# Retention and a squared-ReLU feed-forward in one kernel: groups of two batches, weight transfers issued closer together, and early masks on VectorE

## The chip, the cores and the metric

The kernel runs on one core of a Trainium2 chip. The metric is the device time of one execution in microseconds. Before the change it is 292.26 us, the median of three runs (291.97 to 292.5). The profiled execution, from which all lines below come, spans 290.6 us.

## The reference

Eight batches of eight heads are put through a causal retention: scores of q and k are multiplied by a mask that decays with the distance of two positions, and the result is multiplied with v. The heads of a token are then laid side by side into a row x of 512 numbers, and x goes through two matrix products with relu squared between them.

```python
batch, n_heads, seq, head_dim = (8, 8, 576, 64)
n_tokens, d_model, d_ff = (4608, 512, 2048)

scores = scale * np.matmul(q, k.transpose(0, 1, 3, 2))
gamma = 1.0 - 2.0 ** (-5.0 - np.arange(H))
rel = pos[:, None] - pos[None, :]
Dmat = np.where(rel >= 0, gamma[:, None, None] ** rel[None, :, :], 0.0)
ret = np.matmul(scores * Dmat, v)

x = ret.transpose(0, 2, 1, 3).reshape(B * S, H * D)
h = x @ w_in
r = np.maximum(h, 0.0)
out = (r * r) @ w_out
```

## The kernel before

A sequence of 576 positions is four full chunks of 128 rows and a tail of 64; the tails of two batches share one unit of 128 rows. The kernel so has 36 units, taken two at a time as 18 groups. A group's retention works within the chunk (scores `psc`, mask, times v) and adds what earlier chunks left in a state `R` of 128 x 256 numbers. `psS` holds the sums of k times v from which the next state is made: `Rm` at half a chunk, then `R` at its end, multiplied by the decay of 128 positions. The sum of both parts, `psO`, times a row decay is `xT`, the input of the feed-forward: `ph` (x times w_in), `rl` (relu), `gT` (square), `po` (times w_out). From group 2 on the second product is done with seven block products instead of eight, with sums of blocks of gT (`gS`) and differences of blocks of w_out (`wT`).

```python
    units = []
    for bp in range(B // 2):
        for b in (2 * bp, 2 * bp + 1):
            units += [("full", b, c) for c in range(4)]
        units.append(("tail", 2 * bp, 4))
```

So one batch's chunks follow one another, and a group is mostly two chunks in a row of one batch. The states of the two are updated one after the other, because the second needs the first:

```python
            def fr0(s=s, u=u, c0=c0):
                ... Rm = psS[:, 0] (+ R of unit u - 1)         # 128 x 256, VectorE
            def fr1(s=s, u=u):
                ... stmp = psS[:, 1] + Rm                      # 128 x 256, VectorE
            def fr2(s=s, u=u):
                ... R = stmp * dec128                          # 128 x 256, VectorE
```

The first eight units (two batches, groups 0 to 3) are loaded as pairs, `pair`, and go through another form of the retention, in which casts to fp16 are shared among engines (`kx`, `qx`, `vx`), TensorE transposes k and q (`psT`, copied to `kqT`), and masks `rx` are applied in four halves a group. In groups 0 and 1 (`SHARED`) one half of two is copied from PSUM by ScalarE and multiplied by GpSimd:

```python
                if a and g in SHARED:
                    c = add("ACT", -60 + e, 0.66, fc, deps=[t])
                    reads = ms + [c]
                    ms.append(add("POOL", -60 + e, 0.75, fp, deps=[c]))
                else:
                    ms.append(add("DVE", base + 5 + e, 0.66, fm, deps=[t] + ms))
```

The weights come as eight transfers of 1 MB of fp32, cast to fp16 on the way, w0 to w3 for w_in and w4 to w7 for w_out. GpSimd issues them, between its own computing:

```python
            tile_of["w", i] = nc.gpsimd.dma_start(out=dst, in_=src)
        issue = add("POOL", -70 + i, 1.0, fn, deps=issues[-1:], lag=1.6 if issues else 0.0)
        if not issues:
            gate.setdefault(("vx", 0), []).append(issue)
```

The load of k for unit 4 is made to wait until weight 6 has landed:

```python
            if (name, u) == ("k", 4):
                tc.add_manual_dep(t.ins, tile_of["w", 6].ins.name, ..., reason="the weights come first")
```

The order of instructions on each engine is fixed when the kernel is built, by a list scheduler in the program: `add(engine, key, duration, function, deps, acq)` gives it a task with a rank and an assumed duration. On the chip an engine takes its instructions in that order and waits for what each of them needs. TensorE's idle time at the start is filled with products of a zero tile (`warm`, 28 of them).

In the feed-forward a block is eight ph products of 256 columns, in one of four PSUM buffers; ScalarE takes the relu, and the square is done by ScalarE or by VectorE:

```python
            on_act = g >= STRASSEN and fb in (SQ_ACT if g < last_g - 1 else SQ_LATE)     # STRASSEN = 2, SQ_ACT = 0 to 6
```

The last group is the last full chunk and the last tail, with the tail first. Each unit's output is stored in halves of 256 columns; a tail's half needs two issues of 64 rows, since its rows lie in two batches.

Of the kernel before, what the change touches and what calls it, by code (L numbers as in the profile page):

```python
# [103 lines left out]
def kernel(  # L104
# [21 lines left out]
    for bp in range(B // 2):  # L126
        for b in (2 * bp, 2 * bp + 1):
            units += [("full", b, c) for c in range(4)]
        units.append(("tail", 2 * bp, 4))
# [8 lines left out]
    groups[-1].reverse()  # L138
# [10 lines left out]
    st_pool = ctx.enter_context(tc.tile_pool(name="st", bufs=6))  # L149
# [12 lines left out]
    junk = const.tile([P, 512], FP16, name="junk")  # L162
# [54 lines left out]
    for hp in range(NP):  # L217
# [7 lines left out]
    WARM = 28  # L225
# [5 lines left out]
    LAG = {"w0": 1.2, "k4": 0.7, "q4": 0.5}  # L231
    LAG_T, LAG_O = 1.5, 5.0
    PAIRED = 8
    SHARED = (0, 1)
    FIRST = ["k0", "q0", "v0", "k2", "q2", "v2", "w0", "w1", "w2", "w3", "w4", "w5", "w6", "w7", "k4", "q4", "v4", "k6", "q6", "v6"]
    sched = Schedule(dict(ff=4, prS=1, prO=1, g=3, ld=5, wst=4, kq=7, v16=7, rT=4, x=3, rl=3, o=4, p1=2, u2=2, u4=2,
                          R=6, Rm=6, kqT=6))
# [38 lines left out]

    def add_load(u):
        kind, b, c = units[u]
        for n, (name, src) in enumerate((("k", k), ("q", q), ("v", v))):
            def fn(name=name, src=src):  # L280
                x = ld.tile([P, H, D], FP32, name=f"{name}32", tag=f"{name}32")
                tile_of[name + "32", u] = x
                if kind == "full":
                    nc.sync.dma_start(out=x, in_=src[b, :, c * P:(c + 1) * P, :].rearrange("h p d -> p h d"))
                else:
                    for i in range(2):
                        nc.sync.dma_start(out=x[i * 64:(i + 1) * 64],
                                          in_=src[b + i, :, 512:576, :].rearrange("h p d -> p h d"))
            loaded[name, u] = dma_task(0, 1.2 if loaded else 2.1, fn, acq=("ld",) if n == 0 else ())

    def add_load_pair(name, u):
        b, c = units[u][1:]
        n = "kqv".index(name)

        def fn():
            if name != "q":
                tile_of["stage", u] = stage.tile([P, 2, H, 2 * D], FP32, name="pair", tag="wst")
            x = tile_of[name + "32", u] = tile_of["stage", u][:, n % 2]
            t = nc.sync.dma_start(out=x, in_=(k, q, v)[n][b, :, c * P:(c + 2) * P, :].rearrange("h (p e) d -> p h (e d)", e=2))
            if (name, u) == ("k", 4):  # L300
                tc.add_manual_dep(t.ins, tile_of["w", 6].ins.name,
                                  mybir.DependencyInfo(mybir.DependencyClass.Sync, mybir.DependencyReason.DATA),
                                  reason="the weights come first")
        loaded[name, u] = loaded[name, u + 1] = dma_task(0, 1.81 if loaded else 2.9, fn, acq=("wst",) if name != "q" else (),
                                                         after=2.1 + LAG.get(name + str(u), 0.0))

    issues = []

    def add_weight(i):
# [6 lines left out]
        issue = add("POOL", -70 + i, 1.0, fn, deps=issues[-1:], lag=1.6 if issues else 0.0)  # L316
        if not issues:
            gate.setdefault(("vx", 0), []).append(issue)
# [18 lines left out]

    def quad(out_, lhsT, rhs, row, col, start=True):
        nc.tensor.matmul(out_, lhsT=lhsT, rhs=rhs, start=start, stop=True, skip_group_check=True,  # L339
                         tile_position=(64 * row, 64 * col))  # L340
# [38 lines left out]
    def add_unit_pair(u, base):  # L379
# [29 lines left out]
        for w in gate.get(("vx", u), []):  # L409
            sched.need(w, xs["v"][0])  # L410
# [24 lines left out]
        T["kvx", u] = xs["k"] + xs["v"]  # L435

    def add_ret_pair(g):
# [50 lines left out]
        sched.free("kq", [t])  # L488
        chain = []
        for s in range(2):  # L490
            src = None if s == 0 and not carry else u + s - 1

            def fr1(s=s, src=src):
                r = tile_of["tmp", u + s] = work.tile([P, NP * D], FP32, name="stmp", tag="stmp", bufs=1)
                nc.vector.tensor_tensor(out=r, in0=rT["sum"][s][:, 0:256], in1=tile_of["R", src], op=ALU.add)

            def fr2(s=s, src=src):
                r = tile_of["R", u + s] = st_pool.tile([P, NP * D], FP16, name="R", tag="R")
                x = rT["sum"][s][:, 0:256] if src is None else tile_of["tmp", u + s]
                nc.vector.tensor_tensor(  # L500
                    out=r.rearrange("p (n d) -> p n d", d=D), in0=x.rearrange("p (n d) -> p n d", d=D),
                    in1=dec128.rearrange("p (n o) -> p n o", o=1).to_broadcast([P, NP, D]), op=ALU.mult)
            if src is not None:
                chain.append(add("DVE", base + 5.5 + s, 0.42, fr1, deps=[t] + chain[-1:] + [T["R", src]]))
                T["Rread", src].append(chain[-1])
                sched.free("ff", chain[-1:])
            chain.append(add("DVE", base + (6.5 if u == 0 else 5.6) + s, 0.5, fr2, deps=[t] + chain[-1:], acq=("R",)))
            if src is None:
                sched.free("ff", chain[-1:])
            T["R", u + s], T["Rread", u + s] = chain[-1], []  # L510

        def inter(other):
            for n in range(2):
                for a, b in ((0, 0), (1, 1), (0, 1), (1, 0)):
                    s = a ^ other
                    if s or carry:
                        x = 2 * n + b
                        put2(s, 4 * n + 2 * a + b, tile_of["R", u + s - 1][half(a), half(x)], kqT(s)[half(a), NP + x, :], a)
# [22 lines left out]
        t = add("PE", base + 24, 0.75, fo2, deps=[t, T["R", u]] + ([T["R", u - 1]] if carry else []))  # L541
        for s in range(2):
            sched.free("kqT", [t])
            sched.free("kq", [t])
            if s or carry:
                T["Rread", u + s - 1].append(t)
# [23 lines left out]

    def states(u):

        kind, b, c = units[u]
        if kind == "tail":
            return {0: ("R", u - 5), 1: ("R", u - 1)}
        return {1: ("Rm", u), 0: ("R", u - 1)} if c else {1: ("Rm", u)}
# [37 lines left out]
    def inter(g, u, other):  # L614
        st = states(u)
        for n in range(2):
            for a, b in ((0, 0), (1, 1), (0, 1), (1, 0)):
                c = a ^ other
                if c in st:
                    x = 2 * n + b  # L620
                    put(g, u, c, 4 * n + 2 * a + b, tile_of[st[c]][half(a), half(x)],
# [29 lines left out]
    def out1_deps(g):  # L651
        return [T[x] for u in units_of(g) for x in states(u).values()]

    def after_scores(g, t, key):
        for s, u in enumerate(units_of(g)):
            def fm(s=s, u=u):
                r = tile_of["rT", u] = work.tile([P, 2, NP, 64], FP16, name="rT", tag="rT")
                nc.vector.tensor_tensor(  # L658
# [6 lines left out]
    def after_sums(g, t, key, res):  # L665

        chain = []
        for s, u in enumerate(units_of(g)):
            if u not in full_of(g):
                continue  # L670
            c0 = units[u][2] == 0

            def fr0(s=s, u=u, c0=c0):
                r = tile_of["Rm", u] = st_pool.tile([P, NP * D], FP16, name="Rm", tag="Rm")
                x = tile_of["psS", g][:, 0, cols(s)]
                if c0:
                    nc.vector.tensor_copy(out=r, in_=x)
                else:
                    nc.vector.tensor_tensor(out=r, in0=x, in1=tile_of["R", u - 1], op=ALU.add)

            def fr1(s=s, u=u):
                r = tile_of["tmp", u] = work.tile([P, NP * D], FP32, name="stmp", tag="stmp", bufs=1)
                nc.vector.tensor_tensor(out=r, in0=tile_of["psS", g][:, 1, cols(s)], in1=tile_of["Rm", u], op=ALU.add)

            def fr2(s=s, u=u):
                r = tile_of["R", u] = st_pool.tile([P, NP * D], FP16, name="R", tag="R")
                nc.vector.tensor_tensor(
                    out=r.rearrange("p (n d) -> p n d", d=D), in0=tile_of["tmp", u].rearrange("p (n d) -> p n d", d=D),
                    in1=dec128.rearrange("p (n o) -> p n o", o=1).to_broadcast([P, NP, D]), op=ALU.mult)
            r0 = add("DVE", key + 0.1 + s, 0.42, fr0, deps=[t] + chain[-1:] + ([] if c0 else [T["R", u - 1]]),  # L690
                     acq=("Rm",))
            if not c0:
                T["Rread", u - 1].append(r0)
            r1 = add("DVE", key + 0.2 + s, 0.42, fr1, deps=[r0])
            r2 = add("DVE", key + 0.3 + s, 0.5, fr2, deps=[r1], acq=("R",))
            chain += [r0, r1, r2]
            T["Rm", u], T["R", u], T["Rread", u], T["Rmread", u] = r0, r2, [], r1
        if chain:
            sched.free(res, [chain[-2]])

    def after_outs(g, t1, t2, key):
        us = units_of(g)
        n = len(us)
        for u in us:
# [3 lines left out]
            for name, ru in states(u).values():  # L708
                if name == "R":
                    T["Rread", ru].append(t2)  # L710
                else:
                    sched.free("Rm", [t2, T["Rmread", u]])
# [22 lines left out]
    def add_ret(g):  # L735
# [17 lines left out]
        if joined(g):  # L753
# [6 lines left out]
            def f2():  # L760

                emit_sums(g + 1, "prS")
                emit_out2(g)
# [4 lines left out]
                     deps=[t1] + T["masked", g] + T["masked", g + 1] + sums_deps(g + 1), acq=("prS",))  # L768
# [17 lines left out]
    wT = [const.tile([P, HF, HM], FP16, name=f"wT{i}") for i in range(4)]  # L786
# [36 lines left out]
    def add_ff(g):  # L823
# [10 lines left out]
        for fb in range(NF // nf):  # L834
# [16 lines left out]
            on_act = g >= STRASSEN and fb in (SQ_ACT if g < last_g - 1 else SQ_LATE)  # L851
# [185 lines left out]
    for u in range(NU):  # L1037
        if ("Rread", u) in T:
            sched.free("R", T["Rread", u])
# [33 lines left out]
```

## Time and profile before

| | us |
|---|---|
| time, median of three runs | 292.26 |
| span of the profiled execution | 290.6 |
| TensorE busy | 281.6 |
| VectorE busy | 197.9 |
| ScalarE busy | 183.0 |
| GpSimd busy | 91.4 |
| first ph product starts | 17.88 |
| ph products that need the last quarter of w_in start | 26.77 |
| first ph product of group 2 starts | 54.04 |
| last product ends, by the model | 287.0 |

The profile calls the engines PE (TensorE; PEld is its weight load), DVE (VectorE), ACT (ScalarE), POOL (GpSimd) and SP (SyncE), and POOLq or SPq their queues, which issue transfers. In a group of instructions, out<-in are tile names, and x is a count. The chain of waits follows the work that ended last back to its releasers; in order of time it reads as a diary of what was waited for. Windows give each engine's busy time in a stretch. TensorE's busy time in them includes the warm-up products, and counts a product as busy until its modelled end.

| stretch, us | PE | DVE | ACT | POOL |
|---|---|---|---|---|
| 0 to 10 | 8.64 | 4.32 | 5.45 | 4.86 |
| 10 to 20 | 8.09 | 9.72 | 6.02 | 8.72 |
| 20 to 30 | 9.04 | 6.11 | 5.01 | 3.71 |
| 30 to 40 | 10.00 | 4.94 | 5.27 | 0.00 |
| 40 to 50 | 9.92 | 8.51 | 6.42 | 5.16 |
| 50 to 60 | 9.40 | 8.49 | 4.59 | 5.05 |

### The profile page before, as it was taken

How to read it: one execution, taken by the hardware profiler on the slowest of the kernel's cores; microseconds unless marked ns; L12 is line 12 of the kernel's file. 1: busy time of each engine (PE TensorE's matmuls, PEld its weight loads, DVE VectorE, ACT ScalarE, POOL GpSimd, SP SyncE). 2: the span in 40 equal slices, each digit the busy share in tenths (PEclk: the TensorE clock that was granted, in tenths of full speed). 3: DMA queues.
4: the chain of work that ended last, by engine and by line, in shares of the span. 5: the costliest groups of instructions: out<-in, count | busy, mean ns of one | idle time of the engine just before them, and what ended most of it. 6: DMA issues, size and time to landing. Idle time of an engine off the chain costs nothing.

```text
span 290.6 us, 10028 instructions
## 1 busy us (share of the span) xinstructions
PE 281.6 (97%) x4316; PEld 233.6 (80%) x4316; DVE 197.9 (68%) x427; ACT 183.0 (63%) x351; POOL 91.4 (31%) x125
## 2 busy tenths in 40 slices
PE   8978999999999999999999999999999999999995
PEld 3557755688888888888888888888888888888884
DVE  3895369949384849675968767867767876565632
ACT  5654466486767575867767566666767676747830
POOL 5782035525433334241604251615051500000000
PEclk9999999999999999999999999999999999999999
DMA  7999999999999999997959999969699820201004
GB/s 200 275 192 181 182 300 280 215 204 193 235 173 220 208 167 235 219 214 182 190 135 210 200 192 213 204 170 187 161 182 212 167 74 2 74 2 73 2 0 147
DMA packets 139421, 49.94 MB, mean 172 GB/s; under 512 B 118128, under 2 KB 135024, under 8 KB 139376
## 3 DMA queue, kind: packets, MB, share of 16 engines
q1 hardware_dynamic: 134848, 44.84, 75.1%
q0 software_dynamic: 4224, 4.19, 9.1%
q8 instruction: 34, 0.56, 0.8%
q10 hardware_dynamic: 304, 0.26, 0.3%
q14 instruction: 11, 0.09, 0.1%
HBM read 36.70 MB, written 9.44 MB: 159 GB/s over the span
## 4 chain that ended last, share of the span: by engine, by line
PE 88%; DVE 6%; DMA 3%; ACT 1%; issue 1%; POOL 0%; DVEq 0%
PE ph L841 41%; PE po L933 34%; PE psO L339 4%; PE po L881 3%; DMA w_in<-in_moe_w_in_dram 3%; DVE rx L459 2%; PE warm L248 2%; PE psS L339 2%; PE psc L339 2%; DVE vx L396 2%; DVE R L500 1%; PE psT L417 1%; DVE xT L552 0%; ACT rl L849 0%; POOL rx L466 0%
## 5 line engine op out<-in xcount | busy, mean ns | idle before, releaser
L841 PE MATMUL ph<-xT,w_in 128*128 128x256 f16 x1152 | 140.1, 273 | 1.1 <-DMA w_in<-in_moe_w_in_dram 1.1
L841 PEld LDWEIGHTS <-w_in 128*128 128x128 f16 x1152 | 110.6, 98 | 16.6 <-DMA w_in<-in_moe_w_in_dram 1.9
L849 ACT ACTIVATE rl<-ph 128x512 f16<-128x512 f32 x144 | 84.9, 590 | 57.2 <-PE ph L841 55.8
L859 ACT ACTIVATE gT<-rl 128x512 f16<-128x512 f16 x104 | 65.6, 631 | 3.0
L933 PEld LDWEIGHTS <-gS 128*128 128x128 f16 x512 | 49.5, 98 | 6.1 <-DVE gS L910 0.2
L933 PE MATMUL po<-wT,gS 128*128 128x256 f16 x384 | 52.1, 273 | 0.0
L910 DVE TENSOR_TENSOR gS<-gT,gS 128x512 f16<-128x512 f16 x64 | 32.6, 515 | 13.4 <-ACT gT L859 12.7
L933 PEld LDWEIGHTS <-gT 128*128 128x128 f16 x384 | 37.3, 98 | 4.4
L910 DVE TENSOR_TENSOR gS<-gT 128x512 f16<-128x512 f16 x64 | 33.5, 524 | 10.7 <-ACT gT L859 10.5
L933 PE MATMUL po<-w_out,gT 128*128 128x256 f16 x256 | 34.7, 273 | 0.0
L363 POOL TENSOR_TENSOR v<-v,vdec_full 128x512 f16<-128x512 f32 x24 | 26.4, 1100 | 21.7 <-DMA v<-in_v_dram 12.2
L351 POOL CAST kq<-k 128x512 f16<-128x512 f32 x28 | 19.5, 696 | 42.3 <-DMA k<-in_k_dram 40.6
L351 POOL CAST kq<-q 128x512 f16<-128x512 f32 x28 | 19.1, 682 | 42.3 <-DMA q<-in_q_dram 42.3
L861 DVE TENSOR_TENSOR gT<-rl 128x512 f16<-128x512 f16 x40 | 19.5, 489 | 17.6 <-ACT rl L849 17.2
L956 DVE TENSOR_TENSOR o<-po,u 128x256 f32<-128x256 f32 x31 | 13.0, 420 | 14.8 <-PE po L933 9.6
L719 DVE TENSOR_TENSOR xT<-psO,gam_full 128x512 f16<-128x512 f32 x28 | 18.1, 684 | 6.8 <-PE psO L339 6.8
L946 ACT COPY u<-po 128x256 f32<-128x256 f32 x32 | 11.8, 368 | 17.2 <-PE po L933 17.0
L658 DVE TENSOR_TENSOR rT<-psc,mask 128x512 f16<-128x512 f32 x28 | 18.3, 682 | 3.9 <-PE psc L339 3.9
L933 PE MATMUL po<-w_out,gS 128*128 128x256 f16 x128 | 16.9, 273 | 0.0
L933 PE MATMUL po<-wT,gT 128*128 128x256 f16 x128 | 16.6, 273 | 0.0
L881 PE MATMUL po<-w_out,gT 128*128 128x512 f16 x64 | 15.8, 380 | 0.0
L956 DVE TENSOR_TENSOR o<-po,p 128x256 f32<-128x256 f32 x17 | 7.2, 423 | 12.5 <-ACT u L946 6.5
(81 smaller groups left out, 239.6 us busy)
## 6 DMA issues: line engine op xcount, KB each, us to landing
out_dram<-o SPq DMA_DIRECT2D x31, 256.0 KB, 3.5
k<-in_k_dram SPq DMA_DIRECT2D x24, 256.0 KB, 4.4
q<-in_q_dram SPq DMA_DIRECT2D x24, 256.0 KB, 5.0
v<-in_v_dram SPq DMA_DIRECT2D x24, 256.0 KB, 4.9
pair<-in_k_dram SPq DMA_DIRECT2D x4, 512.0 KB, 5.9
pair<-in_q_dram SPq DMA_DIRECT2D x4, 512.0 KB, 6.0
pair<-in_v_dram SPq DMA_DIRECT2D x4, 512.0 KB, 7.0
w_in<-in_moe_w_in_dram POOLq DMA_DIRECT2D x4, 512.0 KB, 7.7
```

The costliest lines, as they stand in the source:

```text
L339: nc.tensor.matmul(out_, lhsT=lhsT, rhs=rhs, start=start, stop=True, skip_group_check=True, tile_position=(64 * row, 64 * col))
L351: op(out=out_.rearrange("p (n b a d) -> p n b a d", n=2, b=2, a=2), in_=in_.rearrange("p (n a b) d -> p n b a d", n=2, a=2))
L363: nc.gpsimd.tensor_tensor(out=t, in0=tile_of["v32", u], in1=vdec[kind].rearrange("p (h o) -> p h o", o=1).to_broadcast([P, H, D]), op=ALU. ...
L658: nc.vector.tensor_tensor(out=r, in0=tile_of["psc", g][:, :, cols(s)].rearrange("p a (n i) -> p a n i", i=64), in1=mask.rearrange("p (o r ...
L841: nc.tensor.matmul(tile_of["ph", g, fb][:, j, :], lhsT=w_in16[:, m, fi * P:(fi + 1) * P], rhs=tile_of["x", g][:, m, :], start=(m == 0), st ...
L849: nc.scalar.activation(out=t, in_=tile_of["ph", g, fb], func=ACTF.Relu)
L859: nc.scalar.activation(out=t, in_=rl, func=ACTF.Square)
L861: nc.vector.tensor_tensor(out=t, in0=rl, in1=rl, op=ALU.mult)
L881: nc.tensor.matmul(tile_of["po", u], lhsT=tile_of["g", g][:, fi, s * P:(s + 1) * P], rhs=w_out16[:, fi, :], start=(fi == 0), stop=(fi == N ...
L910: nc.vector.tensor_tensor(out=Sx(k, h), in0=in0(h), in1=in1(h), op=op)
L933: nc.tensor.matmul(tile_of["pb", g, bank], lhsT=left(i), rhs=right[:, i, :], start=(start and i == 0), stop=(i == HF - 1), skip_group_chec ...
L956: nc.vector.tensor_tensor(out=o_tile(u)[:, half * HM:(half + 1) * HM], in0=bank(x), in1=tile_of[name, g], op=ALU.add)
```

## The change

From unit 8 on, two batches advance together: a group is the same chunk of two batches, so both states are updated by one instruction of 512 columns. Tails come two units at a time, after each second pair of batches, as groups of their own (8 and 17). The weights' issues get higher rank and shorter lags, the first is tied to the landing of v for unit 0 and no longer follows GpSimd's first product, and k for unit 4 waits for weight 5. All masks of groups 0 and 1 are VectorE's, and in exchange squares of groups 0 and 1 go to ScalarE. The warm-up products become 34 and read a weight tile not yet in use. The last group's order is no longer reversed.

```diff
-        for b in (2 * bp, 2 * bp + 1):
-            units += [("full", b, c) for c in range(4)]
-        units.append(("tail", 2 * bp, 4))
+        bs = (2 * bp, 2 * bp + 1)
+        units += [("full", b, c) for c in range(4) for b in bs] if bp else [("full", b, c) for b in bs for c in range(4)]
+        if bp % 2:
+            units += [("tail", b, 4) for b in (2 * bp - 2, 2 * bp)]
...
-    groups[-1].reverse()
...
-    junk = const.tile([P, 512], FP16, name="junk")
+    wT = [const.tile([P, NF // 2, DM // 2], FP16, name=f"wT{i}") for i in range(4)]
+    junk = wT[3][:, 0:2].rearrange("p f m -> p (f m)")
...
-    WARM = 28
+    WARM = 34
-    LAG = {"w0": 1.2, "k4": 0.7, "q4": 0.5}
+    LAG = {"k4": 0.7, "q4": 0.5}
-    SHARED = (0, 1)
+    SHARED = ()
-                          R=6, Rm=6, kqT=6))
+                          R=5, Rm=2, kqT=6))
...
             if (name, u) == ("k", 4):
-                tc.add_manual_dep(t.ins, tile_of["w", 6].ins.name, ...)
+                behind(t, tile_of["w", 5])
...
-        issue = add("POOL", -70 + i, 1.0, fn, deps=issues[-1:], lag=1.6 if issues else 0.0)
-        if not issues:
-            gate.setdefault(("vx", 0), []).append(issue)
+            if i == 0:
+                behind(tile_of["w", i], tile_of["load", "v", 0])
+        issue = add("POOL", -90 + i, 0.9, fn, deps=issues[-1:] or [loaded["v", 0]], lag=1.0 if issues else 0.0)
...
-            on_act = g >= STRASSEN and fb in (SQ_ACT if g < last_g - 1 else SQ_LATE)
+            on_act = fb in (SQ_ACT if g < last_g - 1 else SQ_LATE)
...
-        for s, u in enumerate(units_of(g)):          # Rm, stmp and R for one unit after the other, 256 columns
...
+        def fr0():                                   # Rm, stmp and R for both units, 512 columns
+            r = tile_of["Rm", g] = st_pool.tile([P, 2, NP * D], FP16, name="Rm", tag="Rm", bufs=2)
+            ...
+        def fr1():
+            r = tile_of["tmp", g] = work.tile([P, 2, NP * D], FP32, name="stmp", tag="stmp", bufs=1)
+            nc.vector.tensor_tensor(out=flat(r), in0=tile_of["psS", g][:, 1], in1=flat(tile_of["Rm", g]), op=ALU.add)
+        def fr2():
+            r = tile_of["R", g] = st_pool.tile([P, 2, NP * D], FP16, name="R", tag="R", bufs=5)
+            decay(flat(r), flat(tile_of["tmp", g]))
```

Where a group has only tails, it makes no psS, and the first product of the joined step before it waits for that group's masks (`first_waits` in the kernel).

In the order of instructions that each engine gets, VectorE has 46 instructions fewer (429 to 383), ScalarE 14 squares more and four copies fewer, GpSimd four products fewer, and TensorE the same products plus the six warm-ups. On SyncE's queue the load of v for unit 6 now stands ahead of the first two stores; before it stood behind the first.

## The prediction

> **What bounds the kernel now.** I read the engine table of the page first, then the chain of waits in order of time, then the waits and the transfers by stretch.
>
> ```profile
> PE 281.6 (97%) x4316; PEld 233.6 (80%) x4316; DVE 197.9 (68%) x427; ACT 183.0 (63%) x351; POOL 91.4 (31%) x125
> ```
>
> TensorE leads, but "97% busy" counts the warm-up products and modelled ends, so I counted work. A 256-column product follows the next after 0.109 us (16 in 1.75 us of the chain), a 512-column one after 0.216 us, a 64x64 one after about 0.0095 us. Products counted in stretches of 10 us at these prices give 8.1 us of work for 20-30, 9.0 for 40-50, 8.1 for 50-60, and 9.7 to 10.2 for nearly every stretch from 60 to 280. So the **steady part is full**: 1008 + 896 products of 0.109 us make 208 of the 228 us from 57.2 to 285.5, and 1680 small ones make 16 more. Only the ramp (0 to 58 us) and the end (after 286 us) have time to give. The chain through the ramp:
>
> ```profile
> 14.26 1.96 DVE vx L396
> 16.27 0.41 PE psS L339 x28
> ...
> 16.95 0.59 ACT rx L463
> 17.62 1.07 POOL rx L466
> 18.73 7.99 DMA w_in<-in_moe_w_in_dram
> 26.77 2.79 PE ph L841 x24
> ```
>
> Columns: start, length, what. The last quarter of w_in lands at 26.7, 8 us after GpSimd issued it, and GpSimd issued it so late because it first multiplied masks (L466). From 26.77 on the chain is TensorE without a gap until 41.5, then TensorE and VectorE in turn, up to here:
>
> ```profile
> 49.28 1.27 DVE vx L396
> ...
> 50.73 1.35 DVE xT L552 x2
> 52.08 1.16 DVE rx L459 x2
> 53.24 0.34 DVE stmp L495
> ...
> 53.61 1.26 DVE R L500
> 54.88 1.21 DVE rx L459 x2
> ...
> 56.13 0.75 PE psO L339 x40
> ```
>
> Here VectorE sets the pace of units 4 to 7. The third view is the SyncE queue's own waits:
>
> ```profile
> SPq L299 <- DMA w_out<-in_moe_w_out_dram: 25.9, 1, 25.9
> ```
>
> The load of k4 stands 25.9 us behind weight 6 and goes out at 34.4. The last is DMA by stretch (the last two columns are share and GB/s):
>
> ```profile
> 23.00:25.00 2.00, 1.74 (x17) 1.34 (x15) 1.12 (x3) 1.00 (x2) 0.70 (x1) 1.00 1.11 140
> 27.00:34.00 7.00, 7.00 (x59) 5.52 (x57) 2.52 (x6) 3.04 (x6) 0.00 (x0) 1.00 1.24 205
> ```
>
> With the weights queued the engines move 205 GB/s; in 23-25 they fall to 140, in 15-17 to 165, and in 35-36 to 89, where neither weights nor loads are queued.
>
> [...]the trace has 0.414 to 0.424 for the 256-wide state updates and 0.68 for the 512-wide masks[...]. [...]L500[...] takes 1.39 us at 12.54, beside GpSimd's masks (11.34 to 13.63), and its like L687 has a median of 0.425. [...]
>
> **The change part by part.**
>
> 1. *Masks of groups 0 and 1.* Four ScalarE copies (4 x 0.59 = 2.4 us) and four GpSimd products (4 x 1.17 = 4.7 us) go; VectorE gets four masks of 0.66 us = 2.6 us. VectorE is 9.7 of 10 us busy in 10-20, so this lies on its path; but without GpSimd's products its updates at 12.54 and 17.81 fall from 1.39 and 1.25 to about 0.43, giving back 1.8 us. The first vx also runs less beside GpSimd (1.23 to about 0.8). The sum is about +0.4 us, and the first ph stays at 17.4 to 17.9.
>
> 2. *Weights.* w0 is issued when v0 has landed, ahead of GpSimd's vx (9.77 to about 8.8). With four GpSimd products gone and the lags shortened, w1 to w3 move from 13.57, 15.59, 18.73 to about 11, 12.5 and 15.4 (the last behind vx of unit 2, which waits for v2 at about 14), the w_out quarters from 20.7-23.7 to about 16-20. Bytes don't shrink: 3.15 MB of loads at 290 GB/s (10.9 us) and 4.19 MB of weights at 203 GB/s (20.7 us), begun at 2.3, end at 33.9 if nothing ever runs dry. What can be won is the lulls: about 0.35 us in 15-17 and 0.75 in 23-25. A quarter takes 2.6 us, so w3, in order, can land at 13.2 + 4 x 2.6 = 23.6 at the earliest. I take 25.2, as [...]the products before it (56 of 0.109 us, 1.3 us of psO, from 17.4) fill TensorE to 24.8 anyway. Gain: 26.8 - 25.2 = **1.6 us**, all on the path.
>
> 3. *k4 behind w5, not w6.* It goes out about 3 to 4 us sooner, the hole at 35-36 closes, and in the order of SyncE's queue v6 now stands ahead of two stores instead of behind one. The chain above waits for v6 (48.9). TensorE lacks about 2.5 us of work in 37-58. I give **0.9 us** to this, with the weight differences wT moved ahead of vx of unit 4, out of the stretch 43-49.
>
> 4. *Squares of groups 0 and 1 on ScalarE.* 14 go from VectorE (0.43 us) to ScalarE (0.63 us): +8.8 us there. With 16 relus of 0.60 that is 18.4 us of ScalarE between about 18 and 37, where it is now busy 10.3 of the 20 us from 20 to 40. Each block of eight ph products (0.87 us) then costs 1.23 us of ScalarE; with four PSUM buffers the last block starts no sooner than the twelfth relu, 18 + 11 x 1.23 + 0.6 = 32.1. TensorE gets there at about 35. It is close, not binding. Cost: **+0.2 us**.
>
> 5. *Two batches in a group.* In each of 12 groups, six updates (2 x 0.41, 2 x 0.42, 2 x 0.52 = 2.7 us) become three of 512 columns (3 x 0.68 = 2.0 us), and the second unit no longer waits for the first. VectorE is freed of 12 x 0.7 = 8 us, but it waits for others there and TensorE is full: **0** on the path. TensorE's small products are the same in number.
>
> 6. *The end.* The last group is now two tails. Each half row-block is stored by two issues of 64 rows. The last was one issue at 287.52 of 0.34 us; two make **+0.4 us**.
>
> 7. *34 warm-up products, not 28*: they fill idle time; 0.
>
> Sum: -1.6 - 0.9 + 0.2 + 0.4 = -1.9; with a little of part 1 left over I write -2.2: 292.26 - 2.2 = about 290.0.
>
> **The rivals.**
>
> *DMA is the true bound of the ramp.* If the slowest DMA engine had no lull, earlier issues change nothing: w1 to w6 land 2.85 us apart (20.1 to 34.4) against 2.6 at the full rate, which speaks for it. The 140 GB/s speaks against it. Then only parts 3 and 6 are left: 291.5 to 292.3.
>
> *ScalarE becomes the bound of the ramp.* If relus and squares in one queue hold PSUM buffers, ph ends no sooner than now (37.2) and the copies of k for unit 4 wait behind them. For it: a quarter of w_in feeds four blocks, two of each group, and so 4.9 us of ScalarE for 2.6 us of transfer; the 16 blocks need 18.4 us, and TensorE wants to be through them in 17.6 (17.4 to 35). Against it: ScalarE may trail by four PSUM buffers. If it binds: 291.5 to 293.
>
> *The steady part gains too.* If freed VectorE time shortened hidden waits, 4 us could come back at most (228 less 208 less 16). For it: quads wait with the release "issue" 43 times, 10.2 us on the weight-load side. Against it: VectorE holds TensorE up for hardly anything after 60 us. It would make 287 to 288.5.
>
> **Range and chances.** The ramp's gain is between 0 and 4 us, the end costs 0.2 to 0.8, the steady part gives -1 to +0.5 either way. Eight in ten: 287.6 to 292.0. Faster by over 2% needs 286.4, that is, all of the ramp and the steady part together: 0.06. Slower by over 2% needs 298.1: only a new wait in every group would do that, 0.02. Within 2%: 0.92.
>
> **What would show it.** Part 2: w3's ph block starts at about 25 instead of 26.77, and no 140 GB/s lull. Part 1: no L466-like row on GpSimd, the update after the second stmp near 0.43 us. Part 3: v6's cast on VectorE starts two to three us before 49.28. Part 4: ScalarE nearly full from 18 to 37; if ph products wait for relus there, it was too much. Part 5: VectorE's busy time near 187 us, ScalarE's near 190, the interval from one psO to the next still about 14.1 us. Part 6: the span ends about 3.5 us after VectorE's last operation instead of 3.1. It is wrong if the time between groups changes, or if the first ph of group 2 (54.04) moves by other than 1.5 to 3.5 us.

## The result, and the profile after

The changed kernel takes **290.75 us**, the median of four runs (290.56 to 290.92), against 292.38 us for the kernel before, run beside it. The ratio is 0.9946, with a 95% interval from 0.9928 to 0.9963. A second comparison, made later, gave 290.70 us and 0.9932 [0.9909, 0.9954]. So the change is worth a little over half a per cent, and the prediction of 290.0 us was 0.75 us too low. The four runs lie within 0.4 us, and the six of the second comparison within 0.3; the 19 of the kernel before in that comparison lie between 291.61 and 294.40.

The engine table of the changed kernel's page (busy time, share of the span of 289.1 us, instructions):

```profile
PE 282.1 (98%) x4322; PEld 234.3 (81%) x4322; DVE 182.4 (63%) x381; ACT 188.2 (65%) x361; POOL 84.1 (29%) x121
```

VectorE lost 15.5 us, GpSimd 7.3, ScalarE gained 5.2, and the span fell by 1.5 us only. TensorE is what it was. The chain of waits shows where the 1.5 us come from (start, length, what):

```profile
10.95 8.72 DMA w_in<-in_moe_w_in_dram
...
19.72 1.49 PE ph L859 x12
...
22.29 5.78 PE ph L859 x52
28.07 0.86 PE po L899 x4
...
52.28 1.75 PE ph L859 x16
54.03 0.68 PE psO L345 x40
```

Set beside the chain of before, two things are gone. The last quarter of w_in is no link any more: only w1 (issued at 10.95) is waited for, and from 19.7 us TensorE works on, with one gap of 0.1 us, until the first po at 28.07. And the VectorE links between 49 and 56 us (vx, xT, rx, stmp, R) have vanished; the stretch up to group 3 is TensorE's alone. The same moments in both kernels, from their traces:

| moment | before | after | difference |
|---|---|---|---|
| first ph | 17.88 | 17.74 | -0.1 |
| first po, behind 80 ph products | 29.56 | 28.07 | -1.5 |
| ph of groups 0 and 1 at their end | 37.39 | 35.90 | -1.5 |
| first ph of group 2 | 54.04 | 52.28 | -1.8 |
| psO of group 3 | 56.13 | 54.03 | -2.1 |
| psO of the last group | 256.62 | 254.44 | -2.2 |
| VectorE's last operation ends | 287.49 | 285.31 | -2.2 |
| span | 290.6 | 289.1 | -1.5 |

The moments are the starts of pieces of the chain; in the repeat of the changed kernel (run 10) the first po came at 28.24 and psO of group 3 at 54.12, so a difference of 0.1 or 0.2 us between two profiles says nothing. Everything is won before 56 us, nothing is won in the 200 us from psO of group 3 to psO of the last group (200.49 before, 200.41 after; the steady part in what follows), and 0.7 us are given back behind VectorE's last operation.

DMA by stretch (window, length, then busy time of PE, PEld, DVE, ACT, POOL, then PEclk, DMA share, GB/s):

```profile
23.00:25.00 2.00, 2.00 (x21) 1.80 (x19) 0.71 (x2) 1.94 (x4) 0.00 (x0) 1.00 1.24 205
27.00:34.00 7.00, 7.00 (x57) 5.31 (x55) 2.41 (x4) 6.84 (x13) 0.00 (x0) 1.00 1.23 215
```

The lull of 140 GB/s at 23-25 us is filled (205), and ScalarE, at 6.84 of 7 us, is nearly full from 27 to 34. Yet no wait of TensorE on a relu appears among its waits. SyncE's queue now waits 21.3 us for a weight ahead of k4 instead of 25.9.

The state updates, from the groups with shapes kept apart (count, then busy time, mean ns, idle time before):

```profile
L445 DVE TENSOR_TENSOR R<-stmp,dec 128x512 f16<-128x512 f32 x12 | 10.0, 831 | 0.4
L705 DVE TENSOR_TENSOR stmp<-psS,Rm 128x512 f32<-128x512 f32 x12 | 8.2, 687 | 0.3
L701 DVE TENSOR_TENSOR Rm<-psS,R 128x512 f16<-128x512 f32 x9 | 6.1, 680 | 0.0
L404 DVE TENSOR_TENSOR vx<-pair,vdec_pair 128x512 f16<-128x512 f32 x4 | 3.2, 791 | 3.0 <-DMA pair<-in_v_dram 3.0
L445 DVE TENSOR_TENSOR R<-stmp,dec 128x256 f16<-128x256 f32 x6 | 2.7, 450 | 0.2
```

Three updates of a group make 0.83 + 0.69 + 0.68 = 2.2 us. The last two rows are the ramp's: vx had a mean of 1369 ns before and R one of 867.

The end (start, length, engine, operation):

```profile
284.89 0.42 DVE L974 TENSOR_TENSOR o<-po,p 128x256 f32<-128x256 f32 x1
282.63 3.83 SPq L833 DMA_DIRECT2D out_dram<-o  x4
```

SyncE issues its last store until 286.46, that is 1.15 us after VectorE's last operation. Before it was done 0.37 us after it. The trace has the two last issues singly: 0.46 and 0.58 us for 64 rows each, where the kernel before has one of 0.34 us, for 128 rows.

### The profile page after: what moved, and what is told of

Same layout as the page of the kernel before. It is cut to its first block, busy times and chain, and to the rows that moved or that the text cites. A ratio compares the mean times of both kernels' runs of the same rounds, so it can differ in the third digit from the quotient of the medians.

```text
span 289.1 us, 9988 instructions
## 1 busy us (share of the span) xinstructions
PE 282.1 (98%) x4322; PEld 234.3 (81%) x4322; DVE 182.4 (63%) x381; ACT 188.2 (65%) x361; POOL 84.1 (29%) x121
## 4 chain that ended last, share of the span: by engine, by line
PE 91%; DMA 3%; issue 2%; POOL 2%; DVE 0%; POOLq 0%; DVEq 0%
PE ph L859 44%; PE po L951 34%; PE po L899 5%; PE psO L345 4%; DMA w_in<-in_moe_w_in_dram 3%; PE psc L345 2%; PE psS L345 2%; PE psT L423 1%; POOL mask L215 0%; POOL vx L404 0%; POOL w_in L319 0%; DVE o L974 0%; POOL mask L207 0%; DVE p L1003 0%; POOL mask L211 0%
## 5 line engine op out<-in xcount | busy, mean ns | idle before, releaser
L877 ACT ACTIVATE gT<-rl 128x512 f16<-128x512 f16 x118 | 74.4, 631 | 3.4
L928 DVE TENSOR_TENSOR gS<-gT 128x512 f16<-128x512 f16 x64 | 30.9, 485 | 12.6 <-ACT gT L877 12.5
L359 POOL CAST kq<-k 128x512 f16<-128x512 f32 x28 | 18.6, 663 | 61.4 <-DMA k<-in_k_dram 60.2
L371 POOL TENSOR_TENSOR v<-v,vdec_full 128x512 f16<-128x512 f32 x24 | 25.4, 1057 | 21.9 <-DMA v<-in_v_dram 20.9
L359 POOL CAST kq<-q 128x512 f16<-128x512 f32 x28 | 18.5, 660 | 30.8 <-DMA q<-in_q_dram 30.6
L879 DVE TENSOR_TENSOR gT<-rl 128x512 f16<-128x512 f16 x26 | 12.8, 492 | 12.6 <-ACT rl L867 11.9
```

Source lines behind the costliest of these rows:

```text
L359: op(out=out_.rearrange("p (n b a d) -> p n b a d", n=2, b=2, a=2), in_=in_.rearrange("p (n a b) d -> p n b a d", n=2, a=2))
L371: nc.gpsimd.tensor_tensor(out=t, in0=tile_of["v32", u], in1=vdec[kind].rearrange("p (h o) -> p h o", o=1).to_broadcast([P, H, D]), op=ALU. ...
L877: nc.scalar.activation(out=t, in_=rl, func=ACTF.Square)
L928: nc.vector.tensor_tensor(out=Sx(k, h), in0=in0(h), in1=in1(h), op=op)
```

## The experiments

All times are compared with the kernel before, run beside them on the same chip; its medians there were 292.43 us for runs 1 to 4, 292.36 for runs 5 to 8, 292.86 for runs 9 and 10, and 292.33 for run 9b. The theory at the start was that of the prediction: the ramp carries the gain, by way of the weights' issues. The rivals were that the grouping of two batches carries it, or that one simpler part of the ramp does. The 34 warm-up products were not tried alone; run 6, which has most of the gain, has 28.

**1. The grouping alone.** The changed kernel with all its ramp taken back:

```diff
-    SHARED = ()
+    SHARED = (0, 1)
-    WARM = 34
+    WARM = 28
-    LAG = {"k4": 0.7, "q4": 0.5}
+    LAG = {"w0": 1.2, "k4": 0.7, "q4": 0.5}
-                behind(t, tile_of["w", 5])
+                behind(t, tile_of["w", 6])
-        issue = add("POOL", -90 + i, 0.9, fn, ..., lag=1.0 if issues else 0.0)
+        issue = add("POOL", -70 + i, 1.0, fn, ..., lag=1.6 if issues else 0.0)     # and its gate on vx of unit 0
-            on_act = fb in (SQ_ACT ...
+            on_act = g >= STRASSEN and fb in (SQ_ACT ...
```

> The changed kernel with every part of the ramp put back (issues and lags of the weights, k4 behind weight 6, masks of groups 0 and 1 shared, their squares on VectorE, 28 warm-up products): what stays is the grouping of two batches, the tails in groups of their own and the last group of two tails. Theory (the gain is all in the ramp, the grouping gives nothing on TensorE's path, the end costs 0.7 us): 0.5 to 0.9 us slower than the kernel before, 292.9 to 293.3; psO of group 3 at about 56.1 and psO of the last full group's successor as far from it as before. Rival (the grouping shortens the steady part by about 1 us, and the ramp brings only the rest): 291.3 or less, with the last product ending about 1 us earlier than before.

Measured: 292.77 us, 1.0009 [0.9995, 1.0023]; the span is 290.9 us, psO of group 3 at 55.56, the steady part 200.77 us. The lull is back:

```profile
15.00:17.00 2.00, 1.38 (x56) 0.94 (x53) 2.00 (x3) 1.07 (x2) 1.56 (x2) 1.00 0.99 148
```

By itself the grouping, which takes 8 us of work from VectorE by the prediction's count, gives nothing: the steady part is no shorter, and the end, 3.74 us behind VectorE's last operation, is 0.6 us longer. That the loss is 0.3 us and not the 0.5 to 0.9 of the theory comes from psO of group 3, which is 0.6 us earlier than in the kernel before although the ramp's edits are out. What moved it was not isolated.

**2. The ramp alone.** The kernel before with all the ramp's edits (those above, the other way round).

> The kernel before with the ramp's parts alone (weights issued early and close, k4 behind weight 5, all masks on VectorE, squares of groups 0 and 1 on ScalarE, 34 warm-up products); units and groups are as before, and so is the last group (tail and full chunk). Theory: the ramp's 2.1 us without the 0.7 us of the end, so about 290.1, 0.6 us faster than the changed kernel. Rival (the grouping carries part of the gain): 291 or more, slower than the changed kernel.

Measured: 291.12 us, 0.9956 [0.9946, 0.9965]. The ramp is as fast as the changed kernel's (psO of group 3 at 54.09), and the last store is issued as soon behind VectorE's last operation as before (0.36 us), though the span ends 0.3 us later behind it (3.40 us). Yet the time is no better than the changed kernel's, since from psO of group 3 to the last it takes 201.46 us, 1.0 us more than before. One wait of TensorE that neither the kernel before nor the changed one has was found (total, times, longest):

```profile
PE po L934 <- DVE gS L911: 0.7, 2, 0.5
```

Its larger part is near 140.7 us, where a sum gS of 1.15 us stands behind six state updates and beside a GpSimd product of v. So by these profiles the grouping is not worthless beside the fast ramp: it makes good up to 1.0 us, and the longer end takes part of that again. How firm that is, run 6 says.

**3. Weight issues and k4 as before, the rest changed.** The issue line, the gate, `LAG` and `behind(t, tile_of["w", 6])` of run 1, with the masks left on VectorE.

> The changed kernel with the weights' issues, their lags and k4 behind weight 6 as before; masks and squares stay as changed. Without GpSimd's mask products the issues still move up a little. Theory (early issue removes the lulls of the transfers, and this is most of the ramp's gain): w0 issued at about 9.8, products of the last quarter of w_in at 25.5 to 26.5, time 291.6 to 292.4. Rival (it is the masks taken off GpSimd that move the weights, the ranks and lags do little): 290.9 to 291.3.

Measured: 291.12 us, 0.9959 [0.9943, 0.9975]; psO of group 3 at 54.12 (54.03 in the changed kernel), no lull between 14 and 33 us (206 GB/s in the mean, 199 to 215 by the microsecond). This fells the theory in its first form. The edits on the issues themselves, and k4 behind w5, are worth 0.1 us of the ramp at most; the changed kernel's own repeat has the same 54.12. The medians differ by 0.4 us, with intervals that overlap.

**4. Masks of groups 0 and 1 shared again, the rest changed.**

```diff
-    SHARED = ()
+    SHARED = (0, 1)
```

> The changed kernel with the masks of groups 0 and 1 shared with ScalarE and GpSimd again; weights and squares stay as changed. Theory (GpSimd's four products of 1.17 us stand between the issues[...], but the new ranks already put most issues ahead of them): the first xT ends about 1 us later, the first weights land about as now, time 291.0 to 291.8. Rival (the masks are the key to the ramp): 292.2 or more, with a lull in the transfers again between 15 and 25 us. ScalarE has four copies more in a stretch where it is nearly full; if that binds, products of groups 0 and 1 wait for relus.

Measured: 294.26 us, 1.0066 [1.0045, 1.0088]; 3.5 us above the changed kernel. The weights kept flowing (206 GB/s at 15-17 us, 201 at 23-25), with the last quarter of w_in landed at 24.76, but the masks came late. TensorE's waits, and the chain:

```profile
PE psO L345 <- POOL rx L481: 1.5, 3, 0.9
```

```profile
12.64 1.82 DVE R L445
14.46 0.80 DVE qx L408
...
15.76 1.53 DVE vx L404
17.29 1.27 DVE xT L573 x2
...
18.70 1.91 PE ph L859 x16
20.61 0.38 PE psc L345 x16
...
21.00 0.70 DVE rx L474
...
21.73 0.59 ACT rx L478
...
23.53 1.16 POOL rx L481
...
24.73 0.58 PE psO L345 x28
```

It was not the issues that the masks of group 1 waited for: GpSimd had issued w5 by 19.0 us and then stood idle for 3.4, until ScalarE's copy. The chain goes back over that copy, VectorE's mask and psc, which in this order comes behind 16 ph products, to VectorE, where R took 1.82 us beside GpSimd's masks (0.42 in run 6) and the first ph so came at 18.70, 1.0 us later than in the changed kernel. Before, the issues waited for the masks; here TensorE does. Runs 3 and 4 with the two kernels make a table of four. The gain is in the step from the left column to the right, and the lower row is harmless only there. (The upper left is the kernel before, which differs from run 3 also in grouping, squares and warm-ups; run 6 makes the upper step with the masks alone, from 292.4 to 291.14.)

| | masks shared with GpSimd | masks on VectorE |
|---|---|---|
| issues as before | 292.4 (292.8 with the grouping, run 1) | 291.12 (run 3) |
| issues closer together | 294.26 (run 4) | 290.75 (the changed kernel) |

**5. The end on two queues.** In the changed kernel the two issues of the last two half row-blocks go out one on SyncE's queue and one on ScalarE's.

```diff
-                eng.dma_start(out=out[r0:r0 + 64, lo:hi], ...)
+                (eng[i] if isinstance(eng, tuple) else eng).dma_start(out=out[r0:r0 + 64, lo:hi], ...)
-                    eng = ("ACT", ...) if d is d11 or d is d22 else ("SP", ...)
+                    eng = ("ACT", ...) if d is d11 else ("SP", ...)
-                    nc.scalar if eng[0] == "ACT" else nc.sync
+                    nc.scalar if eng[0] == "ACT" else nc.sync if lo and u == uA else (nc.sync, nc.scalar)
```

> The changed kernel with the two issues of each of the last two half row-blocks put on two queues, SyncE's and ScalarE's, instead of both on one. Theory (the changed end is 0.7 us longer because the last half is stored by two issues one after the other on SyncE's queue, each about 0.55 us): the span ends 3.1 to 3.4 us after VectorE's last operation instead of 3.8, 290.1 to 290.4, 0.4 to 0.7 us faster than the changed kernel. Rival (the landing of small transfers, not their issue, is what takes longer): no change, 290.7.

Measured: 290.48 us, 0.9926 [0.9896, 0.9955]. The span ends 3.44 us after VectorE's last operation, where it was 3.79, a little longer than the theory had. Run 10 takes this up.

**6. Masks alone.** The kernel before with one edit, the one of run 4 the other way round.

> The kernel before with one edit: masks of groups 0 and 1 all on VectorE. Theory (GpSimd without its four products issues the weights in time by itself; ranks, lags, k4 and squares add nothing): weights issued between 10 and 20 without lulls, psO of group 3 at 54.1 to 54.5, time 291.0 to 291.5. Rival (VectorE is full in 10 to 20 and 40 to 57 and needs the squares taken off it): psO of group 3 at 55.5 or later, 292 or more.

Measured: 291.14 us, 0.9952 [0.9937, 0.9967]. GpSimd's timeline (start, length, what) with no other edit:

```profile
11.43 0.76 POOL L315 DMA_DIRECT2D w_in<-in_moe_w_in_dram  x1
14.21 1.23 POOL L396 TENSOR_TENSOR vx<-pair,vdec_pair 128x512 f16<-128x512 f32 x1 [2.02 <-DVE R L500]
15.39 1.55 POOL L315 DMA_DIRECT2D w_in<-in_moe_w_in_dram  x2
16.92 2.98 POOL L315 DMA_DIRECT2D w_out<-in_moe_w_out_dram  x4
```

w1 goes out at 11.43 instead of 13.57, w3 at about 16.2 instead of 18.73, w_out from 16.92 instead of 20.67, nearly as in the changed kernel (w3 at 15.54, w_out from 16.34). The stretch 23-25 has 206 GB/s. psO of group 3 is at 54.51: of the 2.1 us that the ramp gains, 1.6 come from this line. In time it is 1.2 of the 1.6 us; what the other edits add to it together is not clear of noise (0.9952 against 0.9946 and 0.9932, with intervals that overlap).

The traces also say by what way. From w1's landing on the chain is TensorE's alone:

```profile
20.31 1.48 PE ph L841 x12
...
22.87 5.78 PE ph L841 x52
28.66 0.86 PE po L881 x4
```

In the kernel before TensorE was no further behind up to there: the first ph of the two kernels is at 17.88 and 17.72, and psO of group 1, the product behind the shared masks, began at 21.12 there and only at 21.72 here. So it was neither late masks nor a slowed VectorE that held the kernel before up. It was the last two quarters of w_in, landed at 23.46 and 26.72 instead of 22.77 and 25.31, for which TensorE stood idle 0.26 and 0.47 us. At the first po the difference is 0.9 us (29.56 to 28.66). The other 0.7 come behind the early ph, where the VectorE links of 46 to 56 us are gone here as well: the weights end 1.4 us sooner, so k4, still behind w6, goes out at 32.99 instead of 34.41. This is read from the two traces; no run holds back w3 or k4 alone.

The same run says something of the steady part. From psO of group 3 to the last psO it took 201.32 us, though TensorE's and VectorE's instructions from group 2 on stand in exactly the order of the kernel before, which took 200.49; TensorE waited 0.6 us for gS there, as in run 2. Run 9a, with that same order after psO of group 3, took 200.94, and 9b, whose ramp is slow, 200.74. The kernels with two batches in a group lie between 200.1 and 200.9. But the profiled execution of run 6 took 291.89 us, 0.75 more than the median of that run, and that of run 2 0.42 more; only that of 9a is at its median. So the old grouping behind a fast ramp may lose half a microsecond in the steady part, or up to 1.0 in some executions, and one profile of each kernel is not enough to say more. The spread points the same way: the 22 executions of run 6 lie between 290.43 and 292.21 us, those of the changed kernel between 290.56 and 290.92. The cause is not the order of instructions; it may be how GpSimd's products fall beside VectorE (the gS of 1.15 us in run 2 had one beside it, where the median is 0.42), which no run isolates.

**7. Squares alone.** The kernel before with the squares of groups 0 and 1 on ScalarE.

```diff
-            on_act = g >= STRASSEN and fb in (SQ_ACT ...
+            on_act = fb in (SQ_ACT ...
```

> The kernel before with one edit: squares of groups 0 and 1 on ScalarE. Masks stay shared, so ScalarE gets 14 squares of 0.63 us beside its four copies. Theory (squares are beside the path; they make room on VectorE that nothing needs): 292.0 to 292.6, no difference. Rival (ScalarE in its order holds the mask copies or PSUM buffers up): 293 or more, group 1's masks late.

Measured: 292.13 us, 0.9983 [0.9967, 1.0]; psO of group 3 at 56.02, the lulls as before. Not told from nothing.

**8. Squares back on VectorE in the changed kernel.**

> The changed kernel with the squares of groups 0 and 1 on VectorE again (0.43 us each). Theory: no difference, 290.6 to 290.9, psO of group 3 at 54.0 to 54.3. Rival (VectorE's relief lets the weight differences wT and vx of unit 4 come early, and that is what shortens the stretch 37 to 57): 291.2 or more, with vx of unit 4 and masks of group 2 later.

Measured: 291.40 us, 0.9954 [0.9940, 0.9969]; psO of group 3 at 54.39, 0.36 us later than in the changed kernel. VectorE is then busy 10.5 us of 18 to 37 instead of 7.5. The time is in the rival's range, but its sign is weak: the first mask of group 2 comes 0.2 us later (44.61 for 44.37). The squares on ScalarE so seem to help a little once the weights come early, though the intervals of the two times overlap.

**9. Is it GpSimd's queue?** Two runs asked by what way the products on GpSimd delay the weights. The first, 9a, is run 6 with four idle tasks on GpSimd.

```diff
+    idle = const.tile([P, 320], FP32, name="idle")
...
+                if a and g in (0, 1):
+                    def fi():
+                        for _ in range(3):
+                            nc.gpsimd.iota(idle, pattern=[[1, 320]], ...)
+                    c = add("ACT", -60 + e, 0.01, lambda: None, deps=[t])
+                    add("POOL", -60 + e, 0.75, fi, deps=[c], lag=0.65)
```

> The kernel before with the masks of groups 0 and 1 on VectorE (as in the run that did only this, 291.14 us), plus four tasks of GpSimd that compute nothing that is used (three iotas of 128x320 each[...]) where the products of the masks stood in GpSimd's order. Theory A, the time that the products took of GpSimd's queue between weight issues is what delayed the weights: the lulls near 15-17 and 24-25 us come back, psO of group 3 at 55.3 us or later, time 291.9 us or more. Theory B, what mattered was the products' hold on the mask itself (its latency through ScalarE and GpSimd, or the slowing of VectorE beside them), not the queue: no lulls, psO of group 3 near 54.5, time 291.0 to 291.4 us.

Measured: 291.58 us, 0.9974 [0.9948, 1.0], between both expectations. GpSimd's timeline, and DMA in the first of the two stretches:

```profile
11.32 2.75 POOL L473 IOTA idle<- 128x320 f32 x6
14.02 0.77 POOL L316 DMA_DIRECT2D w_in<-in_moe_w_in_dram  x1
...
15.80 1.55 POOL L316 DMA_DIRECT2D w_in<-in_moe_w_in_dram  x2
17.35 2.76 POOL L473 IOTA idle<- 128x320 f32 x6
```

```profile
15.00:17.00 2.00, 0.90 (x56) 0.74 (x57) 1.48 (x4) 1.07 (x2) 2.00 (x3) 1.00 1.12 147
```

The two idle tasks ahead of w1, three iotas each, took 2.75 us and bring back the lull at 15-17 (147 GB/s; 204 in run 6). That much is shown: time in GpSimd's order ahead of an issue makes a lull, here with work that no mask waits for. But the lull costs next to nothing:

| us | before | run 6 | run 9a | changed |
|---|---|---|---|---|
| w1 issued, landed | 13.57, 20.09 | 11.43, 20.26 | 14.02, 20.27 | 10.95, 19.68 |
| w3 issued, landed | 18.73, 26.72 | 16.19, 25.31 | 16.60, 25.37 | 15.54, 24.71 |
| w_out's first quarter issued | 20.67 | 16.92 | 20.05 | 16.34 |
| k4 issued | 34.41 | 32.99 | 33.37 | 29.90 |
| first po | 29.56 | 28.66 | 28.67 | 28.07 |
| psO of group 3 | 56.13 | 54.51 | 54.88 | 54.03 |

w1, issued 2.6 us later than in run 6, landed at the same time, and so did w3; the first po did not move. The 0.4 us by which psO of group 3 is later come behind it, by way of k4, 0.4 us later, and VectorE, which is on the chain again from 43.88 to 49.74. The other pair of tasks fell behind w3, where in the kernel before a product stood ahead of it, and the stretch 23-25 keeps 196 GB/s. So what the kernel before loses at the first po is not the early lull; w3 was delayed here by only 0.4 us, and its share, which the traces of run 6 name, is not tested by this run.

The second, 9b, holds products at the old places. Run 6 again, with products on GpSimd that nothing reads, and w3 and the first quarter of w_out made to follow them.

```diff
+                if a and g in (0, 1):
+                    c2 = add("ACT", -60 + e, 0.66, ...)              # half of psc copied to a tile of its own
+                    p2 = add("POOL", -60 + e, 0.75, ..., deps=[c2])  # multiplied by the mask twice, read by nobody
+                    if g == 1:
+                        sched.need(issues[3 + e], p2)
+                        ...                                          # no lag; the second product behind w3
+                    ms.append(c2)                                    # the other mask comes behind the copy
```

> The kernel before with the masks of groups 0 and 1 on VectorE (291.14 us by itself), and beside them four products on GpSimd whose results nothing reads (each two halves of 256 columns, fed by a ScalarE copy of psc), held at the very places of the kernel before: two between the casts of unit 0 and w1, one between w2 and w3, one between w3 and the quarters of w_out. No mask that TensorE or VectorE reads waits for them. Theory A, the products cost time by standing in GpSimd's in-order queue ahead of weight issues: w3 goes out at 18 us or later and its ph starts at 26 or later, the lulls at 15-17 and 23-25 us are back, psO of group 3 at 55.5 us or later, 292.0 to 292.8 us. Theory B, they cost time by making the masks late or by slowing VectorE: none of that, 291.0 to 291.5 us.

Measured: 293.46 us, 1.0042 [1.0028, 1.0055], beyond what either theory expected. GpSimd and TensorE's clock (the third number from the right in the second fence):

```profile
16.02 0.80 POOL L316 DMA_DIRECT2D w_in<-in_moe_w_in_dram  x1
19.84 1.50 POOL L476 TENSOR_TENSOR shadow<-shadow,mask 128x256 f16<-128x256 f16 x2 [3.02 <-ACT shadow L472]
21.28 0.80 POOL L316 DMA_DIRECT2D w_in<-in_moe_w_in_dram  x1
```

```profile
20.00:23.00 3.00, 3.00 (x16) 2.13 (x14) 2.96 (x7) 0.77 (x2) 2.82 (x5) 0.50 0.97 152
```

GpSimd stood 3.0 us idle with w3 behind a product that waited for its copy, and w3 went out at 21.28, 2.6 us later than in the kernel before. Products that nobody reads so hold the weights up, which is the direction of theory A. The size can't be used. The copies came late because VectorE's cast of q, 0.42 us in run 6, took 1.93 us at 14.45, beside a GpSimd product, TensorE ran dry at 15-17 us (0.56 of 2 us busy), and its granted clock then was 0.50, from 17.45 to 24.28 us (in the mean 0.58 from 17 to 20, 0.50 from 20 to 23, 0.68 from 23 to 25). A mask of VectorE, too, waited for such a copy (0.47 us at 19.78). So more causes of loss than one are in this run, and they are not told apart.

**10. The changed kernel and the split end, side by side.**

> The changed kernel unaltered, on the same chip as the next one, so that the two can be set against each other: 290.75 us within 0.3, ratio to the kernel before 0.994 to 0.996.

> The changed kernel with the two output issues of each of the last two half row-blocks on two queues, again. If one issue of about 0.55 us is saved behind VectorE's last operation: 0.3 to 0.5 us below the changed kernel of the same call, about 290.3 us. If its lower time in the earlier run was chance: equal to it within 0.15 us.

Measured: 290.70 us, 0.9932 [0.9909, 0.9954] for the changed kernel, 290.56 us, 0.9926 [0.9903, 0.9949] with the split end. The tail behind VectorE's last operation is again shorter, 3.56 us instead of 3.74, and the span 288.7 instead of 289.1. In the traces the last store lands 2.24 (run 5) and 2.36 us after VectorE's last operation, and 2.60 and 2.59 in the two profiles of the changed kernel, so the issue does set the landing. Over both comparisons the split saves 0.1 to 0.3 us of the median; the 0.14 us of the second is what the expectation called chance. It beats the kernel before; that its time beats the changed kernel's is not shown, as the runs of the two overlap.

## Why the prediction was right, and where its terms were off

The time lies in the range, and the gain was 1.6 us where 2.3 were expected. The mechanism holds: masks off GpSimd, weights issued and landed sooner, ramp shorter. But there was luck in the number. The range began only 0.3 us below the kernel before and was 4.4 us wide; three terms of the sum were mis-sized, and their errors partly cancel; and the last step, from -1.9 to -2.2 "with a little of part 1 left over", has nothing behind it, as part 1's own sum is a cost of 0.4 us. Without it the forecast is 290.4.

- **Part 1, masks, "about +0.4" for VectorE and the first ph unmoved.** Right: first ph 17.88 to 17.74. R of the ramp is back to 450 ns in the mean, close to the 0.43 named for it. A mask on VectorE took 0.68 us (L459 of the kernel before, median), where the term has 0.66.
- **Part 2, weights, -1.6.** Right in size: the products that need w3 start at 25.29 instead of 26.77 (25.2 was named, the author's estimate), and the first po moved by -1.5. The quarters from w1 to w6 land 2.53 us apart instead of 2.85. The attribution was only half of it. The text named "four GpSimd products gone and the lags shortened"; the first alone gives 0.9 us at the first po (run 6), the second at most 0.1 (run 3, 28.22). The rest came with the other edits; the squares, too, could be taken out alone at little cost (28.31 in run 8). Shortened lags with the products still there cost 3.5 us (run 4).
- **Part 3, k4 behind w5, -0.9.** Too large, and won by another edit. k4 did go out 4.5 us sooner (29.90), v6's cast on VectorE came 1.7 us sooner, at 47.56, and from the end of the early ph to psO of group 3 it took 0.6 us less (18.13 for 18.74). But run 6, with k4 still behind w6, has that too (18.02): the weights end sooner there. The failed step is the hole at 35-36. It was not free of transfers (the last quarter of w_out landed at 36.89, k4 was issued at 34.41), and filling it set nothing that TensorE waited for: in run 3, with k4 behind w6, k4 was issued 2.7 us later than in the changed kernel, at 32.56, and landed at the same time (36.88; 36.84), while the last quarter of w_out landed 0.4 us sooner (35.04; 35.48).
- **Part 4, squares, +0.2.** Its claim was "close, not binding", and that held: ScalarE is busy 17.0 of the 19 us from 18 to 37, and TensorE waits for no relu. The cost was 0, or a gain of 0.3 to 0.4 us at psO of group 3 (run 8, against the two profiles of the changed kernel); by what way is not shown.
- **Part 5, grouping, 0.** Against the kernel before that is what the steady part shows (200.49 and 200.41), and run 1 too. Against the fast ramp with the old grouping the profiles give 0.5 to 1.0 us (runs 2, 6 and 9a), which the prediction did not see; two of them are of executions well above their medians, so this is not firm. An update group took 2.2 us, not 2.0: R at 512 columns has a mean of 0.83 us, with a median of 0.69 and one of 1.58.
- **Part 6, the end, +0.4.** It cost 0.7. The term counted one more issue at 0.34 us, the length of one of 128 rows; the two of 64 rows took 0.46 and 0.58 us, so the queue's last issue ends 1.15 us after VectorE instead of 0.37.
- Of the signs named, ScalarE's busy time (188.2 for 190) and group 2's first ph (-1.8, within 1.5 to 3.5) were right; VectorE's came out at 182.4 instead of 187, since its early operations with GpSimd beside them fell more than counted, vx by 4 x 0.58 = 2.3 us and the 256-column R by 6 x 0.42 = 2.5, and gS fell by 2.4, while the state updates of groups of two batches gave 6.4 us and not 8.

Of the rivals, "DMA is the true bound of the ramp" fell with the filled lulls, "ScalarE becomes the bound" with TensorE's missing waits, and "the steady part gains too" with 200.41 us.

## What to carry to other kernels

GpSimd here issued transfers and also computed, with one order for both: in run 9b, w3 went out behind a product that had waited 3.0 us for its copy. With such an engine, look at what stands ahead of each issue, and move computing off it before tuning ranks and lags. With the computing still there, issues closer together cost 1.8 us against the kernel before (run 4). Ask of a lull whether a landing moves that something waits for: the one at 15-17 us moved none up to the first po (run 9a). In a bundle of edits, try each alone and take each out alone: here one line was most of the gain. Work taken from an engine that nobody waits for gave nothing here: of the 15 us that VectorE lost, the 6 us of the grouping showed in no time by themselves (run 1).

## What the runs showed of the hardware that was not expected

- Idle work of 2.75 us on GpSimd ahead of a weight issue was enough to let the transfers fall from 204 to 147 GB/s at 15-17 us (runs 6 and 9a); the transfer so delayed by 2.6 us landed at 20.27 instead of 20.26.
- In run 9b the granted clock of TensorE was 0.50 from 17.45 to 24.28 us, after a stretch in which it was busy 0.56 of 2 us, with one idle time of 1.63 us. In run 9a it was busy 0.90 of 2 us there, with none longer than 0.76 us, and the clock stayed at 1.00. What made the difference was not tried.
- Half the rows did not make a shorter issue on SyncE's queue: 0.46 and 0.58 us for two stores of 64 rows at the end of the changed kernel, 0.34 us for one of 128 rows before.
- k for unit 4, issued at 29.90 and at 32.56 us, landed at 36.84 and 36.88 (the changed kernel and run 3).
